# Two more items of a linear-attention and MLP kernel in float32 on unsplit weights, and six weight splits moved to later steps

## The chip, the cores and the metric

The kernel runs on one core of a Trainium2 chip. The metric is the device time of one execution in microseconds (us), lower is better. Five engines of the core are spoken of: PE (matrix products), DVE (elementwise and reductions), ACT (activation functions, copies), POOL and SP (here mostly issuing DMAs). Each works through its own list of instructions in order, and they wait for each other through semaphores.

## What is computed

The reference is a linear attention followed by a two-layer MLP without bias:

```python
q_s = softmax(q, over the head dimension)        # q, k, v: (8, 8, 576, 64)
k_s = softmax(k, over the sequence)
x   = q_s @ (k_s^T @ v)                          # per batch and head, then (4608, 512)
h   = x @ w_in                                   # w_in (512, 2048)
g   = h * erf(softplus(h))
out = g @ w_out                                  # w_out (2048, 512), out float32
```

The softmax subtracts the maximum and adds 1e-9 to the sum. The weights arrive as float64 and are decoded to float32 in the kernel.

## The kernel before

**Items.** The tokens are taken in four pairs of batches. Each pair has 1152 tokens, which are three blocks of 384, so there are twelve blocks. The hidden width of 2048 is taken in four groups of 512. One block with one group is an *item*: 48 items, numbered in the order of the list `seq` (line 893), block by block and, inside a block, group 0 to 3. So items 0 to 3 are block 0, items 4 to 7 are block 1, items 8 to 11 are block 2. An item consists of tokens that the author writes as letters: `m` the first product (x with w_in), which leaves H; `T` softplus, `G` erf and `U` the product of both with H, which leave g; `I` and `O` the split of g into two float16 parts; `M` the second product (g with w_out), which adds into three accumulator banks o0 to o2 per block. After a block's last item the banks are copied out (`ob`) and stored.

**Two ways of multiplying.** Items 0 to 3 (`n < NG`, NG is 4) use float32 matmuls on the decoded weights as they are: `mm1_32` (line 975) does sixteen of 384 columns into the PSUM banks pX, pY, pZ, pX, copied out by ACT (line 989), and `mm2` does twelve of 512 columns at line 1061. All later items use float16 parts: every operand is a high part and a low part, and a product is hi times hi, hi times lo and lo times hi. The first product of these items (`mm1`, line 922) is in addition a seven-product scheme for 2 by 2 blocks: seven products, `prod` (line 939), of twelve matmuls with 192 columns each at line 946, put together by four DVE operations (lines 958, 960, 968, 971) and three ACT copies (963, 965, 973). Its tokens are in four steps m*n*.0 to m*n*.3. The second product is 36 matmuls of 512 columns at line 1070.

**Splits.** For that the weights are split once. There are eight jobs (`JOBS`), numbered 0 to 7: w_in group 0, w_in 1, w_out 0, w_in 2, w_out 1, w_in 3, w_out 2, w_out 3. `D` decodes a job into a staging place; `Z` (`wscales`, line 251) computes the scales once all jobs are decoded; `S` (`wsplit`, line 300) and `R` (`wsplit_sums`, line 324) write the float16 parts. A part is made by `split2` (line 293): ACT writes the high part (line 294), then DVE the low part (line 295). For a w_in job S makes two such pairs and then four subtractions on DVE (line 320) in the staging place, and R two more pairs from the sums. A staging place of job j lies in the tile of job j+2, so job j+2 can be split only when job j is done; jobs 6 and 7 are staged in a spare x tile (`sg`) and in `rw`. The token block x of block 1 and later is split in the same way by `finish` (line 370, tokens `f`): an even f makes the parts of x itself, an odd f makes four subtractions (line 386) in place and then two pairs, into the tile `x7`.

**Order.** Up to item 3 and the first splits the order of the tokens is written out in `ORDER`; after it a loop over n from 4 emits `U` of item n-1, the four `m` of item n with `I`, `O` of item n-1 and `M` of item n-2 between them, the splits that the table `SPLITS` lists for n, and then `T` and `G` of item n. `A` and `pace` advance the attention of the coming batches by one step. The recording layer may place instructions of one engine in a somewhat different order than the tokens; each engine then works through its list strictly in that order. Items 0 to 3 are scaled by 1 in softplus (line 1014); later ones by `unit` (line 992), and `gmul` (line 1020) multiplies by GA, made in `wscales`.

## Time and profile before

| | us |
|---|---|
| three timed runs | 852.46, 854.15 (median), 856.45 |
| the profiled execution's own time | 854.95 |
| its span, first to last instruction | 852.8 |
| PE busy in the span | 812.2 |
| DVE busy | 640.0 |
| ACT busy | 506.1 |

The profile is one execution. A row of a timeline has the start in us from the span's start, the length in us, engine, line, operation, output and inputs with the buffer numbers left out, shape, type and count; neighbouring instructions of one kind stand in one row, and what ended an idle stretch just before the row stands in brackets. A float32 matmul leaves two records, so x8 in a row are four matmuls. The start of the next row, and not a row's own length, tells how fast an engine went on, since lengths overlap a little.

### The profile page before, as it was taken

What the parts mean: (1) busy time and instruction counts of PE and PEld (TensorE: products, weight loads), DVE (VectorE), ACT (ScalarE), POOL (GpSimd) and SP (SyncE); (2) the same over time, 40 slices, a digit from 0 to 9 for tenths busy, and PEclk for the clock granted to TensorE, in tenths of its full rate; (3) what the DMA queues carried; (4) which work ended last, traced back from release to release, by engine and by line L of the source; (5) the groups of instructions that cost most, each with busy time, mean ns of one, the idle gap of its engine ahead of it and who ended that gap; (6) DMA issues with size and microseconds to landing.
All of it is one profiled execution on the core that took longest, in us unless ns stands there. A gap on an engine that the chain in (4) does not pass through costs nothing.

```text
span 852.8 us, 15390 instructions
## 1 busy us (share of the span) xinstructions
PE 812.2 (95%) x6464; PEld 557.9 (65%) x6464; DVE 640.0 (75%) x913; ACT 506.1 (59%) x636; POOL 18.1 (2%) x37
## 2 busy tenths in 40 slices
PE   3999996799999999999999999999999999999996
PEld 2655546567766677676776677676776776777672
DVE  6999699998888778876886768876876557554543
ACT  2697677757585467556755467456665565543532
POOL 2101100000000000000000000000000000000000
PEclk9999998899999999999999999999999999999999
DMA  9975820031217212511062212511041000100100
GB/s 271 404 176 175 201 63 26 1 89 34 71 44 137 50 51 50 128 41 26 14 150 55 63 38 61 120 38 26 21 92 13 30 10 1 38 1 1 38 1 38
DMA packets 141348, 61.55 MB, mean 72 GB/s; under 512 B 130528, under 2 KB 132576, under 8 KB 141280
## 3 DMA queue, kind: packets, MB, share of 16 engines
q1 hardware_dynamic: 139104, 52.18, 24.9%
q0 software_dynamic: 2176, 8.39, 2.9%
q8 instruction: 51, 0.84, 0.4%
q14 instruction: 17, 0.14, 0.1%
HBM read 45.09 MB, written 9.44 MB: 64 GB/s over the span
## 4 chain that ended last, share of the span: by engine, by line
PE 64%; DVE 20%; ACT 6%; DMA 4%; issue 3%; SPq 2%; POOL 0%; ACTq 0%; DVEq 0%
PE o L1070 31%; PE pX L946 16%; PE pZ L946 8%; PE pY L946 3%; DVE G L1025 2%; ACT G L342 2%; ACT L342 2%; DVE wt L295 2%; SPq L407 2%; PE x L652 2%; PE kv L540 2%; DVE H L1042 1%; DMA vbuf<-in_v_dram 1%; DMA wt<-in_moe_w_out_dram 1%; DVE wt L214 1%
## 5 line engine op out<-in xcount | busy, mean ns | idle before, releaser
L1070 PE MATMUL o<-wt,H 128*128 128x512 f16 x1584 | 365.6, 379 | 1.9 <-DVE H L1038 1.3
L946 PEld LDWEIGHTS <-wt 128*128 128x128 f16 x3696 | 312.1, 99 | 44.1 <-issue 17.4
L1070 PEld LDWEIGHTS <-H 128*128 128x128 f16 x1584 | 152.5, 98 | 157.5 <-DVE H L1038 1.8
L946 PE MATMUL pX<-x,wt 128*128 128x192 f16 x2112 | 207.2, 249 | 11.9 <-DVE H L968 5.3
L342 ACT ACT_TABLE_LOAD x105 | 134.7, 1283 | 6.2 <-DVE U L996 2.4
L1025 DVE SCALAR_TENSOR_TENSOR G<-G,small,H 128x1536 f32<-128x1536 f32 x44 | 79.9, 1816 | 48.3 <-ACT G L342 48.0
L973 ACT COPY H<-pX 128x384 f32<-128x384 f32 x44 | 20.9, 476 | 147.6 <-PE pX L946 145.1
L946 PE MATMUL pZ<-x,wt 128*128 128x192 f16 x1056 | 104.6, 247 | 0.0
L342 ACT ACTIVATE G<-H,U 128x768 f32<-128x768 f32 (+1 forms) x60 | 72.8, 1231 | 22.1 <-DVE H L971 21.5
L1042 DVE TENSOR_TENSOR H<-G,H 128x1536 f16<-128x1536 f32 x44 | 77.2, 1754 | 1.0
L342 ACT ACTIVATE G<-G 128x1536 f32<-128x1536 f32 x48 | 71.2, 1484 | 0.5
L946 PE MATMUL pY<-x,wt 128*128 128x192 f16 x528 | 51.7, 246 | 1.4 <-DVE H L958 1.4
L441 ACT ACTIVATE x<-x 128x384 f32<-128x384 f32 (+1 forms) x52 | 17.7, 387 | 58.1 <-PE x L652 55.7
L971 DVE TENSOR_TENSOR H<-pZ,H 128x384 f32<-128x384 f32 x44 | 24.2, 549 | 31.4 <-PE pZ L946 31.4
L958 DVE COPY H<-pY 128x384 f32<-128x384 f32 x44 | 24.3, 552 | 25.7 <-PE pY L946 25.7
L294 ACT ACTIVATE x<-x 128x768 f16<-128x768 f32 (+1 forms) x44 | 33.0, 762 | 16.5 <-DVE x L386 15.8
L1038 DVE CAST H<-G 128x1536 f16<-128x1536 f32 x44 | 42.0, 955 | 0.9
L295 DVE SCALAR_TENSOR_TENSOR x<-x,x 128x768 f16<-128x768 f32 (+1 forms) x44 | 37.3, 849 | 3.6 <-ACT x L294 3.5
L1086 DVE TENSOR_SCALAR ob<-o,V 128x512 f32<-128x512 f32 x29 | 21.7, 747 | 21.6 <-PE o L1070 21.5
L960 DVE TENSOR_TENSOR H<-pX,H 128x384 f32<-128x384 f32 x44 | 24.3, 553 | 13.2 <-PE pX L946 12.7
L452 DVE TENSOR_REDUCE q_m<-q 128x16 f32<-128x1024 f32 x14 | 17.0, 1215 | 18.2 <-DMA q<-in_q_dram 18.1
L968 DVE TENSOR_TENSOR H<-pX,H 128x384 f32<-128x384 f32 x44 | 24.2, 550 | 6.0 <-PE pX L946 5.9
(180 smaller groups left out, 791.4 us busy)
## 6 DMA issues: line engine op xcount, KB each, us to landing
out_dram<-ob SPq DMA_DIRECT2D x32, 256.0 KB, 2.3
vbuf<-in_v_dram SPq DMA_DIRECT2D x60, 128.0 KB, 3.3
q<-in_q_dram SPq DMA_DIRECT2D x56, 128.0 KB, 3.2
k<-in_k_dram SPq DMA_DIRECT2D x56, 128.0 KB, 3.3
wt<-in_moe_w_out_dram POOLq DMA_DIRECT2D x5, 1024.0 KB, 8.7
wt<-in_moe_w_in_dram SPq DMA_DIRECT2D x4, 1024.0 KB, 10.7
wt<-in_moe_w_out_dram SPq DMA_DIRECT2D x2, 1024.0 KB, 15.5
H_raw<-in_k_dram SPq DMA_DIRECT2D x2, 512.0 KB, 4.7
```

Of the source, the lines that this page charges most:

```text
L294: nc.scalar.activation(hi, src, AF.Copy, scale=s)
L295: nc.vector.scalar_tensor_tensor(lo, src, s, hi, op0=ALU.mult, op1=ALU.subtract)
L342: i = nc.scalar.activation(out_, in_, func, **kw)
L946: nc.tensor.matmul(o, w[wl][:, c, a * P:(a + 1) * P], x[:, xl, xi, c, :], start=(new and a == 0 and c == 0 and i == 0), stop=(c == 1 and i ...
L958: nc.vector.tensor_copy(C[0, 0], bank2("Y"))
L960: add(C[0, 0], bank2("X"), C[0, 0], op=ALU.add)
L968: add(C[1, 1], bank2("X"), C[1, 1], op=ALU.add)
L971: add(C[0, 1], bank2("Z"), C[0, 1], op=ALU.add)
L1025: nc.vector.scalar_tensor_tensor(flat(s["G"]), flat(s["G"]), GA[:, g:g + 1], flat(s["H"]), op0=ALU.mult, op1=ALU.mult,)
L1038: nc.vector.tensor_copy(flat(s["gh"]), flat(s["G"]))
L1042: nc.vector.tensor_tensor(flat(s["gl"]), flat(s["G"]), flat(s["gh"]), op=ALU.subtract)
L1070: nc.tensor.matmul(o, s[gt][:, a, ts_], w[wl][:, a, :], start=(first_ and a == 0 and i == 0), stop=(last_ and a == FG - 1 and i == 2),)
```

## The change

Items 4 and 5, the first two of block 1, are now groups 2 and 3 instead of 0 and 1, and both of their products are done in float32 on the unsplit weights (`N32 = 6`); items 6 and 7 are groups 0 and 1 in float16 parts. Softplus of items 4 and 5 is scaled by the batch's `ux`, and their product with H by one new scalar GA32. Such items have no `I` and `O`. The first products of item 4 start before `Z`. Only splits S0, R0, S1, R1 are left in `ORDER`; S2 and S4 come in the loop at n = 6, S6, f2, f3, S3 and R3 at n = 7, S5 and R5 at n = 8, S7 at n = 9. The guard in `wsplit` now asks only that job j-2 is split.

```diff
--- before.py
+++ after.py
@@ -36,11 +36,14 @@
     m0.0 m0.1 D0.0.1 D0.1.1 D1.0 D1.1 m0.2 m0.3 T0 G0 Q0
     D2.0 A m1.0 D2.1 m1.1 U0 m1.2 m1.3 T1 G1 Q1 A A D3.0 M0.0 D3.1 M0.1 M0.2 Q2 U1 A A
     m2.0 D4.0 m2.1 D4.1 m2.2 m2.3 T2 G2 Q3 A A D5.0 M1.0 D5.1 M1.1 M1.2 U2 A A Q4 D6.0
-    m3.0 D6.1 m3.1 D7.0 m3.2 D7.1 m3.3 T3 G3 A A A A A A A A A A Q5 U3 Q6 Q7 Z S0 R0 f0 f1
-    M2.0 M2.1 M2.2 M3.0 M3.1 M3.2 S1 R1 S2
+    m3.0 D6.1 m3.1 D7.0 m3.2 D7.1 m3.3 T3 G3 A A A A A A A A A A Q5 U3 Q6 Q7
+    M2.0 M2.1 M2.2 m4.0 m4.1 Z m4.2 m4.3 T4 G4 M3.0 f0 M3.1 M3.2 S0 R0 m5.0 m5.1 U4 m5.2 m5.3
+    T5 G5 f1 S1 R1
 """
 
-SPLITS = {4: "S3 R3 S4", 5: "S5 R5 S6", 6: "S7"}
+
+N32 = 6
+SPLITS = {6: "S2 S4", 7: "S6 f2 f3 S3 R3", 8: "S5 R5", 9: "S7"}
 
 SHARES = [2.51, 0, 0.16, 0.09, 1.58, 2.43, 1.12, 0.26, 0.29, 0.04, 0.78, 1.12, 0.16]
 LEAD = 2.0
@@ -92,6 +95,7 @@
     make_identity(nc, ident)
     small = cp.tile([P, 48], F32, name="small")
     VW = small[:, 3:4]
+    GA32 = small[:, 32:33]
 
     vbuf = cp.tile([P, 4, TM, D + 1], F32, name="vbuf")
     nc.gpsimd.memset(vbuf[:, :, :, D:], 1.0)
@@ -289,20 +293,24 @@
         nc.vector.tensor_scalar(
             VW, m[:, 2:3], m[:, 3:4], 2.0**20, op0=ALU.mult, op1=ALU.mult
         )
+        nc.vector.tensor_scalar(
+            GA32, m[:, 0:1], m[:, 1:2], 2.0**-20, op0=ALU.mult, op1=ALU.mult
+        )
 
     def split2(src, hi, lo, s):
         nc.scalar.activation(hi, src, AF.Copy, scale=s)
         nc.vector.scalar_tensor_tensor(lo, src, s, hi, op0=ALU.mult, op1=ALU.subtract)
 
-    nsplit = [0]
+
+    split = set()
 
     def wsplit(jn):
 
 
         which, g = wjobs[jn]
         s = w_s[which][:, g:g + 1]
-        assert "all" in wready and not raws and jn == nsplit[0]
-        nsplit[0] += 1
+        assert "all" in wready and not raws and (jn < 2 or jn - 2 in split)
+        split.add(jn)
         if which == "out":
             split2(stg.pop(jn), whalf(jn, 0), whalf(jn, 1), s)
             wdone(jn)
@@ -890,7 +898,10 @@
         )]
 
 
-    seq = [(p, bk, g) for p in range(NP) for bk in range(NBK) for g in range(NG)]
+    seq = [
+        (p, bk, (g + 2 * (p == 0 and bk == 1)) % NG)
+        for p in range(NP) for bk in range(NBK) for g in range(NG)
+    ]
     N = len(seq)
     blk_items = {}
     for n, it in enumerate(seq):
@@ -975,8 +986,8 @@
     def mm1_32(n, a):
 
         s = st[n]
-        jn = wjobs.index(("in", n))
-        w, x = stg[jn].rearrange("p (c f) -> p c f", c=4), xbl[0]
+        jn = wjobs.index(("in", seq[n][2]))
+        w, x = stg[jn].rearrange("p (c f) -> p c f", c=4), xbl[n // NG]
         if a == 0:
             s["H"] = ch.tile([P, FG, T], F32, tag="H", bufs=3, name=f"H_{n}")
         b = "XYZX"[a]
@@ -1010,7 +1021,7 @@
         for o, w, b in spans(n):
             h, sp = s["H"], s["G"]
             h, sp = (flat(t) if w == T else t[:, :, o:o + w] for t in (h, sp))
-            u = 1.0 if n < NG else unit(b, g)
+            u = 1.0 if n < NG else bat[b]["ux"] if n < N32 else unit(b, g)
             act(sp, h, AF.Softplus, chain=in_chain(n), scale=u)
 
     def erf(n):
@@ -1022,11 +1033,13 @@
         if n < NG:
             nc.vector.tensor_tensor(flat(s["G"]), flat(s["G"]), flat(s["H"]), op=ALU.mult)
             return
+        assert "all" in wready
         nc.vector.scalar_tensor_tensor(
-            flat(s["G"]), flat(s["G"]), GA[:, g:g + 1], flat(s["H"]),
+            flat(s["G"]), flat(s["G"]), GA32 if n < N32 else GA[:, g:g + 1], flat(s["H"]),
             op0=ALU.mult, op1=ALU.mult,
         )
-        assert "all" in wready
+        if n < N32:
+            return
 
         hl = flat(s["H"]).bitcast(F16)
         s["gh"], s["gl"] = (
@@ -1055,7 +1068,7 @@
         o = acc[tt]
         jn = wjobs.index(("out", g))
         ts_ = slice(tt * P, (tt + 1) * P)
-        if n < NG:
+        if n < N32:
             w = stg[jn].rearrange("p (a e) -> p a e", a=FG)
             for a in range(FG):
                 nc.tensor.matmul(
@@ -1130,7 +1143,7 @@
         elif c == "Z":
             wscales()
         elif c == "m":
-            (mm1_32 if x[0] < NG else mm1)(*x)
+            (mm1_32 if x[0] < N32 else mm1)(*x)
             emitted.add(("m", *x))
         elif c == "M":
             mm2(*x)
@@ -1148,7 +1161,7 @@
     w_even = sum(SHARES[:9]) + NC4 * sum(SHARES[11:])
     w_odd = w_even + sum(SHARES[9:11])
     per_pair = w_even + w_odd
-    n1 = NG + 3
+    n1 = NG + 4
 
     def pace(at_n):
 
@@ -1165,18 +1178,18 @@
 
     for o in ORDER.split():
         tok(o)
-    fi = [2]
+    fi = [4]
     FIN = 2
-    for n in range(4, N + 2):
+    for n in range(N32, N + 2):
         m0, m1, m2 = n < N, n - 1 < N, n - 2 < N
         if m1:
             tok(f"U{n - 1}")
         for i in range(4):
             if m0:
                 tok(f"m{n}.{i}")
-            if 4 < n <= N and i < 2:
+            if N32 < n <= N and i < 2:
                 tok(f"{'IO'[i]}{n - 1}")
-            if m0 and n % NG == FIN and i < 2 and x_next[0] < NP * NBK:
+            if m0 and n % NG == FIN and n > N32 and i < 2 and x_next[0] < NP * NBK:
                 tok(f"f{fi[0]}")
                 fi[0] += 1
             if m2 and i < 3:
```

On PE, from the second product of item 3 on, the list before is this. Names carry the item or batch in their first number: pY_4 is a bank of item 4, o_0_2 the third accumulator of block 0; x7_1 is the split x of block 1, wt0 holds the split of job 0; each matmul of line 946 has its own LDWEIGHTS.

```order
L1061 MATMUL o_0_2_462<-rw_86,G_3_693 128x512 x4
L946 LDWEIGHTS wt0_91
L946 MATMUL pY_4_886<-x7_1_825,wt0_91 128x192
...
L946 MATMUL pX_4_900<-x7_1_825,wt0_91 128x192
...
L946 MATMUL pZ_4_914<-x7_1_825,wt0_91 128x192
...
L946 MATMUL pY_5_1002<-x7_1_825,wt1_92 128x192
```

And with the change, where x_1 is the unsplit x of block 1, wt5 and wt7 hold the staged w_in groups 2 and 3, and sg_6 the staged w_out group 2:

```order
L996 MATMUL pZ_4_2_839<-x_1_139,wt5_96 128x384 x4
L1074 MATMUL o_0_0_449<-rw_86,G_3_693 128x512 x4
L1074 MATMUL o_0_1_457<-rw_86,G_3_693 128x512 x4
L1074 MATMUL o_0_2_462<-rw_86,G_3_693 128x512 x4
L996 MATMUL pX_5_0_894<-x_1_139,wt7_98 128x384 x4
L996 MATMUL pY_5_1_900<-x_1_139,wt7_98 128x384 x4
L996 MATMUL pZ_5_2_907<-x_1_139,wt7_98 128x384 x4
L996 MATMUL pX_5_3_913<-x_1_139,wt7_98 128x384 x4
L957 MATMUL pY_6_945<-x7_1_862,wt0_91 128x192
...
L957 MATMUL pX_6_959<-x7_1_862,wt0_91 128x192
...
L1074 MATMUL o_4_0_973<-sg_6_653,G_4_851 128x512 x4
```

The float16 products of block 1 that stood right behind item 3 now stand behind the float32 first products of items 4 and 5, and between the second and the third of item 6's seven products (the next row is pX_6 once more, with the last part of x7_1) stands a third of item 4's second product.

On ACT, the two high parts of x7_1 that an odd f makes stood before, among the first splits:

```order
L294 ACTIVATE wt1_92<-wt3_94,small_81 128x512
L1080 COPY ob_3_0_854<-o_0_0_449 128x512
L294 ACTIVATE x7_1_825<-x_1_139 128x768
L294 ACTIVATE wt0_91<-wt2_93,small_81 128x1024
...
L1080 COPY ob_3_1_861<-o_0_1_457 128x512
```

The second of them is in the place of the three dots' end, ahead of every softplus of block 1. With the change they stand around item 5's softplus and erf; the dots leave out a table load and the second high part:

```order
L1000 COPY H_5_893<-pX_5_3_913 128x384
L350 ACT_TABLE_LOAD
L350 ACTIVATE G_5_919<-H_5_893,x0_u_311 128x4x192
L350 ACTIVATE G_5_919<-H_5_893,x1_u_634 128x4x192
L301 ACTIVATE x7_1_862<-x_1_139 128x768
...
L350 ACTIVATE G_5_919<-G_5_919 128x1536
...
L976 COPY H_6_944<-pX_6_959 128x2x192
L301 ACTIVATE wt6_97<-sg_6_653,small_81 128x2048
```

So both stand behind the copy of the last first product of item 5, and the second also behind its erf.

On DVE, the last low part of x7_1 stood before ahead of the split of job 1 and of the first evacuation of item 4:

```order
L295 SCALAR_TENSOR_TENSOR x7_1_825<-x_1_139,x7_1_825 128x768
L295 SCALAR_TENSOR_TENSOR wt1_92<-wt3_94,small_81,wt1_92 128x1024
L295 SCALAR_TENSOR_TENSOR wt1_92<-wt3_94,small_81,wt1_92 128x512
L958 COPY H_4_885<-pY_4_886 128x2x192
L320 TENSOR_TENSOR wt3_94<-wt3_94 128x2x256
L295 SCALAR_TENSOR_TENSOR wt2_93<-wt4_95,small_81,wt2_93 128x2048
```

With the change it stands behind G_5, which is `gmul` of item 5; the dots leave out the rest of f1's subtractions, its first low part and four subtractions of job 3:

```order
L302 SCALAR_TENSOR_TENSOR wt4_95<-wt6_97,small_81,wt4_95 128x2048
L969 COPY H_6_944<-pY_6_945 128x2x192
L394 TENSOR_TENSOR x_1_139<-x_1_139 128x2x192
L971 TENSOR_TENSOR H_6_944<-pX_6_959,H_6_944 128x2x192
...
L1037 SCALAR_TENSOR_TENSOR G_5_919<-G_5_919,small_81,H_5_893 128x1536
L302 SCALAR_TENSOR_TENSOR x7_1_862<-x_1_139,x7_1_862 128x768
L302 SCALAR_TENSOR_TENSOR wt6_97<-sg_6_653,small_81,wt6_97 128x2048
```

The last low part of x7_1 has moved from before block 1's products to behind item 5's whole chain of softplus, erf and gmul.

## The prediction

> **What bounds the kernel now.** I read the page first. PE is busy nearly throughout, and the slices show where it isn't.
>
> ```profile
> PE 812.2 (95%) x6464; PEld 557.9 (65%) x6464; DVE 640.0 (75%) x913; ACT 506.1 (59%) x636; POOL 18.1 (2%) x37
> PE   3999996799999999999999999999999999999996
> DVE  6999699998888778876886768876876557554543
> PEclk9999998899999999999999999999999999999999
> ```
>
> After the start, PE falls below nine tenths only in the seventh and eighth of 40 slices (21.3 us each, so about 128 to 171 us), there its granted clock falls too, and DVE is full. Everywhere else the time is PE's own work. So the change is worth what it recovers in that stage, less the PE work that it adds. The busy times by stretch say more:
>
> ```profile
> core 0: us, PE busy (x) PEld busy (x) DVE busy (x) ACT busy (x) POOL busy (x), PEclk, DMA share, GB/s
> 112.03:128.29 16.26, 15.27 (x46) 7.29 (x45) 16.06 (x41) 11.19 (x18) 0.96 (x1) 1.00 0.24 64
> 128.29:200.55 72.26, 58.48 (x540) 46.10 (x539) 69.49 (x101) 50.40 (x55) 0.63 (x2) 0.91 0.16 38
> 140.12:147.30 7.18, 5.66 (x37) 5.05 (x37) 7.17 (x10) 5.44 (x5) 0.00 (x0) 0.52 0.01 3
> 158.80:164.30 5.50, 5.48 (x32) 4.55 (x32) 5.50 (x9) 1.01 (x2) 0.00 (x0) 0.50 0.00 0
> ```
>
> From 128.29, where block 1's first float16 matmul starts, to 200.55, DVE is busy 69.49 of 72.26 us and PE idles 13.8; in two pieces the clock is half. The PE timeline has the waits in brackets, and DVE ends nearly all of them:
>
> ```profile
> 113.19 0.65 PE L261 MATMUL ws_in<-ident,small 128*128 128x128 f32 x4 [0.99 <-DVE small L255]
> 117.99 10.46 PE L1061 MATMUL o<-rw,G 128*128 128x512 f32 x24
> 128.29 1.15 PE L946 MATMUL pY<-x,wt 128*128 128x192 f16 x12
> 136.71 1.15 PE L946 MATMUL pX<-x,wt 128*128 128x192 f16 x12 [1.79 <-DVE H L960]
> 158.82 2.08 PE L946 MATMUL pX<-x,wt 128*128 128x192 f16 x12 [2.84 <-DVE H L968]
> ```
>
> The evacuations that PE waits for stand in DVE's list behind the splits.
>
> How much of the 72.26 us is work? The counts of the three kinds of matmul in that stretch, and the speed of each in a dense stretch later:
>
> ```profile
> 128.29:200.55 72.26, 38.34 (x374) 34.99 (x374) 0.91 0.16 38
> 128.29:200.55 72.26, 17.68 (x72) 6.80 (x72) 0.91 0.16 38
> 128.29:200.55 72.26, 3.93 (x80) 3.13 (x80) 0.91 0.16 38
> 260.02 0.69 PE L540 MATMUL kv<-vbuf,k 128*64 128x65 f32 x16
> 261.34 1.17 PE L946 MATMUL pX<-x,wt 128*128 128x192 f16 x12
> 268.51 1.15 PE L946 MATMUL pX<-x,wt 128*128 128x192 f16 x12
> 269.50 2.75 PE L1070 MATMUL o<-wt,H 128*128 128x512 f16 x12
> 272.09 1.15 PE L946 MATMUL pZ<-x,wt 128*128 128x192 f16 x12
> 241.34 0.60 PE L519 MATMUL kB<-ident,km 128*128 128x128 f32 x4
> 241.77 1.15 PE L946 MATMUL pX<-x,wt 128*128 128x192 f16 x12
> ```
>
> The first three rows are lines 946, 1070 and 540. Twelve of line 946 go on in 0.99 us (268.51 to 269.50), twelve of line 1070 in 2.59, forty kv records in 1.32, four transposes in 0.43. So the work is 374 x 0.99/12 = 30.9, 72 x 2.59/12 = 15.5, 2 x 1.32 = 2.6, and about 1.4 for thirteen transposes: 50.4 us. The stage loses 72.3 - 50.4 = 21.8 us with unrounded terms, and 0.99 more before it, at ws_in.
>
> **What the change adds on PE.** One float32 first product, and float16 ones beside it:
>
> ```profile
> 90.26 2.75 PE L985 MATMUL pY<-x,wt 128*128 128x384 f32 x8
> 92.84 2.74 PE L985 MATMUL pZ<-x,wt 128*128 128x384 f32 x8
> 95.42 2.74 PE L985 MATMUL pX<-x,wt 128*128 128x384 f32 x8
> ```
>
> A quarter of an item takes 2.58 us, so an item 10.32; in float16 it is seven times 0.99, 6.93. A second product is the x24 row at 117.99, 10.30 us to the next row; in float16 three times 2.59, 7.77. So each of the two items costs 20.62 where it cost 14.70, and both together 11.8 us more. All of it is on PE, and nothing hides it.
>
> **What it takes from DVE.** Two items lose four evacuations, a cast and a subtraction each:
>
> ```profile
> 158.22 0.54 DVE L968 TENSOR_TENSOR H<-pX,H 128x384 f32<-128x384 f32 x1
> 158.69 0.94 DVE L1038 CAST H<-G 128x1536 f16<-128x1536 f32 x1
> 160.03 1.74 DVE L1042 TENSOR_TENSOR H<-G,H 128x1536 f16<-128x1536 f32 x1
> ```
>
> That is 2 x (4 x 0.54 + 0.94 + 1.74) = 9.7 us of DVE. It has a price only through PE's waits, and so isn't a term of its own. ACT's evacuations go from three to four per item, next to nothing. The splits stay eight; their cover is now the 30.9 us of PE work that need no split: the first products of 4 and 5 (20.6) and item 3's second (10.3). The wait of 0.99 at ws_in goes, since item 4's first product stands there and needs only x; its third bank waits for the DVE reduction of ws_out, which I place just in time (a queries' load ahead of it in DVE's list could cost 0 to 1.7).
>
> **What is late next.** Here a new wait is added, and the order shows it. The odd f works in place on block 1's x, so it must wait for item 5's last first-product matmul. Its second high part stands on ACT behind item 5's softplus and erf, and its second low part on DVE behind item 5's gmul. Item 6's third product needs it, and everything on PE is queued behind that product. The chain's pieces:
>
> ```profile
> 183.22 1.58 ACT L294 ACTIVATE x<-x 128x768 f16<-128x768 f32 x2 [1.92 <-DVE x L386]
> 193.03 1.76 ACT L342 ACTIVATE G<-H,U 128x768 f32<-128x768 f32 x2
> 195.11 0.48 ACT L965 COPY H<-pX 128x384 f32<-128x384 f32 x1 [0.32 <-PE pX L946]
> 195.61 1.28 ACT L342 ACT_TABLE_LOAD   x1
> 196.90 1.48 ACT L342 ACTIVATE G<-G 128x1536 f32<-128x1536 f32 x1
> 198.42 1.82 DVE L1025 SCALAR_TENSOR_TENSOR G<-G,small,H 128x1536 f32<-128x1536 f32 x1 [0.17 <-ACT G L342]
> 128.25 0.95 DVE L295 SCALAR_TENSOR_TENSOR x<-x,x 128x768 f16<-128x768 f32 x1
> 133.24 2.35 DVE L295 SCALAR_TENSOR_TENSOR wt<-wt,small,wt 128x2048 f16<-128x2048 f32 x1
> ```
>
> From the end of item 5's first product: copy 0.48, table 1.28, softplus 1.76, first high part 0.79, table to the start of gmul 2.81 (195.61 to 198.42), gmul 1.82, low part 0.95: 9.9 us. Meanwhile PE has two float16 products (1.98) and a third of item 4's second product (3.43), 5.4 us. So PE waits 4.5. DVE could make it longer: behind the first of f1's four subtractions stand the low part of S4 (2.35) and two evacuations before the last subtraction, which ends about 0.5 us after the softplus. I take 4.8 us of idle (bounds 4.4 and 6).
>
> Such a gap costs more than itself. After the 2.84 us at 158.82 the clock was 0.50 for 5.5 us: 2.7 us of work lost. I take the same 2.7 (0 if the clock holds, 3.4 as at 140.12, 7.18 x 0.48). [...]
>
> Behind that wait I followed the three lists on, each operation at its row's length. DVE and ACT stay ahead of PE through the late splits, by a few us mostly; two small waits come up near the first products of block 2, 0.4 at a bank and 0.4 at the attention's queries. I take 0.8 for them, with 0 and 4 as bounds. Block 2's products find their split x ready some 8 us early by that reckoning.
>
> **Sum.** Recovered 21.8 + 1.0; paid 11.8 + 4.8 + 2.7 + 0.8 = 20.1. Gain 2.7 us. The profiled execution took 854.95 (span 852.8 and 2.15 around it), so it would take 852.25; it lies 0.8 above the median of 854.15, and on the median the forecast is 851.45, I say 851.4. With the terms' likely errors (each about 1 to 2 us, not all one way) its own range is 848.6 to 854.2.
>
> **Rivals.** *The clock holds or the chain is covered.* If PE's idle falls so across the clock's decision that it isn't halved, or waits and work overlap better, the gain is 5.4: 848.7. For it: a wait of 0.99 at 113.19 left the clock at 1.00. Against it: two of two stretches with long waits were halved. I give it 0.17.
>
> *A second wait of the same kind, slower than before.* With the change S6, R3, part of S5 and f2 stand in DVE's list ahead of the subtraction of the keys' maximum of batch 2, and the kv products on PE, and all behind them, wait for the exp of these keys. Ahead of it in DVE's list since S6's low part are about 14 us: S6 2.35, low parts from R3, S5 and f2 some 5, evacuations, subtractions and a reduction 7. By my reckoning there are 16.4 us for them, and the keys' chain has about 1 us of slack, so it decides from about 3.4 us of delay on: 8 us late is 4.6 idle and again 2.7 at the halved clock. The gain of 2.7 turns into a loss of 1.9 without the clock and 4.6 with it: 856.0 to 858.8. For it: DVE was busy 69.49 of 72.26 us in this stage before, and the change puts six splits there later. Against it: 9.7 us of DVE work are gone. I give it 0.19, two thirds of that at the upper end.
>
> *The table load brings a drain.* If each switch of tables also waited for ACT to run empty, about as long as the load itself takes (1.28), the two in the chain above would lengthen the wait by 2.6 and leave almost no gain, 854.0. Against it: copy, load and erf stand at 195.11, 195.61 and 196.90, back to back. [...] I give it 0.02.
>
> *The loss only moves.* The order changes, but DVE, which by my reckoning ends item 7 about 8 us later against PE's place than before, hands the rest of the gain back in waits of block 2: about 854.1, chance 0.07. The forecast's own case has 0.55.
>
> **Numbers.** About 0.5% (4.3 us) is what a measurement of this kernel can tell from no change: faster is below 849.9, slower above 858.4. Faster: the first rival, 0.17, and a fifth of the forecast's case, 0.12, together 0.29. Slower: the upper two thirds of the second rival, 0.13. Within: 0.58. The range 847.0 to 857.5 leaves out that upper part and a few hundredths at the low end.
>
> **What would show it.** Right: 128 f32 records at the line of `mm1_32` and 96 at that of `mm2` become 192 and 144; the PE timeline has no wait from 112 to the end of item 5's first products near 148; then one wait of 4 to 6 us, ended by the low part of x7_1 on DVE, and a clock of 0.50 for some 5 us behind it; after it nothing above 1 us to block 2. Wrong: that wait missing or under 3 us with the clock at 1.00 (first rival), a wait at the kv products of batch 2 ended by the exp of k (second), a gap ahead of the table loads (third), or new waits between 200 and 260 us (fourth).

## The result: 846.8 us, below the range

| | median, us (lowest to highest, runs) | ratio to before, 95% interval |
|---|---|---|
| before, beside it | 854.02 (852.46 to 856.45, 4) | |
| changed | 846.8 (846.17 to 847.5, 4) | 0.9913 [0.9887, 0.9939] |
| changed, a second time (e8) | 845.6 (844.91 to 846.46, 4) | 0.9909 [0.9895, 0.9922] |
| changed, a third time (e16) | 845.85 (845.2 to 847.16, 5) | 0.9911 [0.9898, 0.9924] |

Each ratio is to runs of the kernel before on the same chip, beside the runs of its row. The change gains 7.2 us where 2.7 was forecast, and the time lies just outside the range, 0.2 us under its low end. The profiled execution took 847.39 with a span of 845.4, 7.4 us shorter than before's. The page of the changed kernel:

```profile
PE 817.5 (97%) x6336; PEld 554.3 (66%) x6336; DVE 631.9 (75%) x900; ACT 506.6 (60%) x638; POOL 18.1 (2%) x37
PE   3999999999999999999999999999999999999996
DVE  6899689998998869867877769867876657553543
PEclk9999999999999999999999999999999999999999
```

The two low slices of PE are gone, and with them the low clock. PE now has more to do (817.5 against 812.2 us) and still ends earlier. The busy times of the two stretches that answer to 112.03:128.29 and 128.29:200.55, split where the float16 products of block 1 begin:

```profile
112.46:149.21 36.75, 35.91 (x109) 19.21 (x108) 33.62 (x66) 26.40 (x35) 0.96 (x1) 1.00 0.14 40
149.21:190.88 41.67, 41.26 (x330) 27.98 (x329) 40.22 (x58) 32.42 (x36) 0.63 (x2) 1.00 0.15 33
149.21:190.88 41.67, 17.16 (x192) 1.00 0.15 33
```

The third row is line 957 alone, the float16 first products. PE is idle 0.84 us in the first stretch and 0.41 in the second, where it idled 13.8 us before. DVE is still busy nearly all the time (33.62 + 40.22 of 78.42 us), but PE hardly waits for it. How much of this is gained at equal work? At 190.88 the changed kernel has 192 records of line 957 behind it, which with the two items that no longer use that line (168) is 14 short of the 374 that before had at 200.55; that is 14 x 0.99/12 = 1.2 us, and with about 0.5 of transposes it owes 1.7. So before needed 88.5 us for what now takes 78.4 + 1.7 = 80.1: a gain of 8.4 us there. The span is 7.4 shorter: 0.4 had been lost ahead of this stretch, which starts at 112.46 instead of 112.03, and 0.6 is given back behind it.

The PE timeline where the prediction placed its new wait; o<-rw is item 3's second product and o<-sg item 4's, both in float32, and line 957 is item 6's first product:

```profile
125.94 2.82 PE L996 MATMUL pZ<-x,wt 128*128 128x384 f32 x8 [0.84 <-DVE wse_in L272]
128.59 10.46 PE L1074 MATMUL o<-rw,G 128*128 128x512 f32 x24
138.89 2.74 PE L996 MATMUL pX<-x,wt 128*128 128x384 f32 x8
...
149.21 1.15 PE L957 MATMUL pY<-x,wt 128*128 128x192 f16 x12
150.20 1.15 PE L957 MATMUL pX<-x,wt 128*128 128x192 f16 x12
151.19 3.62 PE L1074 MATMUL o<-sg,G 128*128 128x512 f32 x8
...
155.31 1.07 PE L957 MATMUL pX<-x,wt 128*128 128x192 f16 x11 [0.41 <-DVE x L302]
156.21 1.91 PE L1074 MATMUL o<-sg,G 128*128 128x512 f32 x4
157.96 0.25 PE L957 MATMUL pZ<-x,wt 128*128 128x192 f16 x1
158.04 1.91 PE L1074 MATMUL o<-sg,G 128*128 128x512 f32 x4
159.79 1.07 PE L957 MATMUL pZ<-x,wt 128*128 128x192 f16 x11
...
205.15 0.59 PE L660 MATMUL x<-asc,kvbd 128*128 128x512 f16 x2 [1.62 <-DVE asc L639]
```

And what DVE and ACT did there, from the copy of item 5's last first product to the two low parts of x7_1 (line 302):

```profile
149.41 0.48 ACT L1000 COPY H<-pX 128x384 f32<-128x384 f32 x1 [0.94 <-PE pX L996]
149.91 1.28 ACT L350 ACT_TABLE_LOAD   x1
151.21 1.76 ACT L350 ACTIVATE G<-H,x_u 128x768 f32<-128x768 f32 x2
152.88 0.84 ACT L301 ACTIVATE x<-x 128x768 f16<-128x768 f32 x1
...
156.43 0.83 ACT L301 ACTIVATE x<-x 128x768 f16<-128x768 f32 x1
...
152.30 0.55 DVE L394 TENSOR_TENSOR x<-x 128x384 f32<-128x384 f32 x1
...
154.30 0.96 DVE L302 SCALAR_TENSOR_TENSOR x<-x,x 128x768 f16<-128x768 f32 x1
...
156.56 1.82 DVE L1037 SCALAR_TENSOR_TENSOR G<-G,small,H 128x1536 f32<-128x1536 f32 x1
158.29 0.95 DVE L302 SCALAR_TENSOR_TENSOR x<-x,x 128x768 f16<-128x768 f32 x1
```

The chain has the length that was forecast: from the end of item 5's first products at 149.21 to the end of the second low part at 159.24 it takes 10.0 us, where 9.9 was reckoned. But item 6's third product (the row at 155.31) starts 0.05 us behind the *first* low part, which ends at 155.26, 4 us before the second. The half that it needs (j = 1 in the code of `finish`) is the one that is made early: its two subtractions are the second and third of the four, the third is the row at 152.30, and at 152.88, ahead of item 5's erf, ACT begins its high part. What needs the late half is the product after it (pZ), and ahead of its bulk at 159.79 stand two pieces of item 4's second product, 1.8 us each. So the late half is hidden as well.

The waits of PE in the changed kernel from 110 to 260 us (us in total, times, longest):

```profile
PE x L660 <- DVE asc L639: 1.6, 1, 1.6
PE kB L527 <- DVE km L518: 1.2, 1, 1.2
PE pZ L996 <- DVE wse_in L272: 0.8, 1, 0.8
PE pX L957 <- DVE x L302: 0.4, 1, 0.4
```

The evacuations of the float16 first products (H), which held PE up most in before's timeline, are gone from the list. Four short waits are left, 4.0 us together; the first two lie behind 190.88.

### The profile page after: what moved, and what is told of

It is laid out like the page before. It is cut to its first block, busy times and chain, and to the rows that moved or that the text cites. A ratio compares the mean times of both kernels' runs of the same rounds, so it can differ in the third digit from the quotient of the medians.

```text
span 845.4 us, 15123 instructions
## 1 busy us (share of the span) xinstructions
PE 817.5 (97%) x6336; PEld 554.3 (66%) x6336; DVE 631.9 (75%) x900; ACT 506.6 (60%) x638; POOL 18.1 (2%) x37
## 4 chain that ended last, share of the span: by engine, by line
PE 66%; DVE 16%; ACT 10%; DMA 3%; issue 3%; SPq 1%; POOL 0%; ACTq 0%; DVEq 0%; POOLq 0%
PE o L1083 28%; PE pX L957 15%; PE pZ L957 8%; PE o L1074 4%; ACT G L350 3%; PE pY L957 3%; ACT L350 3%; DVE G L1037 2%; PE kv L548 2%; DVE H L1055 2%; DMA q<-in_q_dram 1%; PE x L660 1%; SPq L415 1%; ACT wt L301 1%; DVE wt L302 1%
## 5 line engine op out<-in xcount | busy, mean ns | idle before, releaser
L1083 PE MATMUL o<-wt,H 128*128 128x512 f16 x1512 | 347.4, 379 | 1.8 <-DVE H L1051 1.3
L957 PEld LDWEIGHTS <-wt 128*128 128x128 f16 x3528 | 294.0, 98 | 29.3 <-issue 5.6
L1083 PEld LDWEIGHTS <-H 128*128 128x128 f16 x1512 | 145.9, 98 | 150.8 <-DVE H L1051 1.8
L957 PE MATMUL pX<-x,wt 128*128 128x192 f16 x2016 | 193.9, 246 | 1.8 <-ACT H L976 0.7
L957 PE MATMUL pZ<-x,wt 128*128 128x192 f16 x1008 | 98.2, 246 | 0.0
L350 ACT ACTIVATE G<-H,U 128x768 f32<-128x768 f32 (+1 forms) x56 | 69.3, 1255 | 22.1 <-DVE H L982 21.5
L1055 DVE TENSOR_TENSOR H<-G,H 128x1536 f16<-128x1536 f32 x42 | 73.8, 1756 | 1.0
L957 PE MATMUL pY<-x,wt 128*128 128x192 f16 x504 | 48.4, 246 | 0.0
L1099 DVE TENSOR_SCALAR ob<-o,V 128x512 f32<-128x512 f32 x29 | 21.7, 749 | 21.9 <-PE o L1083 21.8
L996 PE MATMUL pX<-x,wt 128*128 128x384 f32 x96 | 33.9, 488 | 0.0
L971 DVE TENSOR_TENSOR H<-pX,H 128x384 f32<-128x384 f32 x42 | 23.3, 555 | 13.3 <-PE pX L957 12.5
```

The costliest lines, as they stand in the source:

```text
L350: i = nc.scalar.activation(out_, in_, func, **kw)
L957: nc.tensor.matmul(o, w[wl][:, c, a * P:(a + 1) * P], x[:, xl, xi, c, :], start=(new and a == 0 and c == 0 and i == 0), stop=(c == 1 and i ...
L971: add(C[0, 0], bank2("X"), C[0, 0], op=ALU.add)
L996: nc.tensor.matmul(ph[:, :T], w[:, c, a * P:(a + 1) * P], x[:, c, :], start=(c == 0), stop=(c == NC4 - 1),)
L1055: nc.vector.tensor_tensor(flat(s["gl"]), flat(s["G"]), flat(s["gh"]), op=ALU.subtract)
L1083: nc.tensor.matmul(o, s[gt][:, a, ts_], w[wl][:, a, :], start=(first_ and a == 0 and i == 0), stop=(last_ and a == FG - 1 and i == 2),)
```

## The experiments

The theory after this result: the float32 items are cover. They give PE work that needs no split while DVE works off the splits, so the loss of the stage goes; they cost 5.9 us each; and the new wait on the late half didn't come because item 4's second product lies over it and the third product needs the early half. The rivals: the gain comes from putting six splits later; it comes from the DVE work that the two items no longer have; or the new wait was never as dear as reckoned.

**e1, the cover held back.** Item 4's second product (x[0] == 4 is its item) is made to stand behind the last matmuls of both products of item 6 that need the parts of an odd f (`held4`, X and Z for pX and pZ), and item 7's first product behind the last of item 6's pX. The step m6.1 is moved up to stand right behind m6.0. The main part of the edit:

```diff
-            mm2(*x)
+            with ExitStack() as es:
+                if x[0] == 4:
+                    es.enter_context(tc.issue_after(held4["X"].ins))
+                    es.enter_context(tc.issue_after(held4["Z"].ins))
+                mm2(*x)
```

> The changed kernel, with the second product of item 4 held behind the third and fourth of item 6's seven first products, so that PE has nothing to lay over the splits of x. Theory (the forecast wait did not come because item 4's second product and the order of the two halves of f1 cover it): PE now waits 4 to 7 us between its second and fifth product of item 6, ended by the low parts of x7_1, the granted clock falls to about 0.5 for some us behind it, and the time is 6 to 10 us above the changed kernel, 853 to 857. Rival (the clock holds at this place whatever the wait, since float32 work goes ahead of it): the waits alone, 4 to 6 us, clock 1.00, 851 to 853. Rival (PE has slack there): under 849.

Measured: 848.74 us, ratio 0.9939 [0.9924, 0.9954]: some 2 us over the changed kernel, not 6 to 10. That is the number of the last rival (under 849), but not its reason, since PE does wait and its clock does fall, only less than was meant. PE's rows there, and its granted clock (us, busy, PEclk):

```profile
152.36 0.24 PE L957 MATMUL pX<-x,wt 128*128 128x192 f16 x1 [1.97 <-DVE x L394]
153.02 0.65 PE L527 MATMUL kB<-ident,km 128*128 128x128 f32 x4 [0.42 <-DVE km L518]
153.88 1.60 PE L957 MATMUL pX<-x,wt 128*128 128x192 f16 x11 [0.21 <-DVE x L302]
155.89 0.32 PE L957 MATMUL pZ<-x,wt 128*128 128x192 f16 x1 [0.40 <-ACT x L301]
```

```profile
154.00:155.00 1.00, 1.00 (x10) 0.63 0.06 16
...
157.00:158.00 1.00, 1.00 (x11) 0.67 0.00 0
```

The waits are 3.0 us together, and the clock was halved for 3.4 us: means of 0.63 and 0.67 are 0.74 and 0.66 us at 0.50, and the two us between, left out here, are at 0.50 throughout. That cost about 1.5 us of work. Of the 4.5, some 2 show in the end; the 1.6 at the attention's queries isn't in this run's list of waits. The recording layer had laid transposes (kB) ahead and had put the second low part ahead of item 5's gmul on DVE (156.00 and 156.87 there), so that the wait was shorter than the edit was meant to make it. This run doesn't price the predicted situation; e15 below does.

**e2 and e3, how many items.** e2 does all four items of block 1 in float32, e3 one. The tables change with it; the eight weight splits stay, and e2 needs no split x for block 1. The main lines of both edits:

```diff
-N32 = 6
-SPLITS = {6: "S2 S4", 7: "S6 f2 f3 S3 R3", 8: "S5 R5", 9: "S7"}
+N32 = 8
+SPLITS = {6: "S2", 7: "f2 f3 S3 R3", 8: "S4 S5 R5", 9: "S6", 10: "S7"}
...
+N32 = 5
+SPLITS = {5: "S1 R1 S2", 6: "S3 R3 S4", 7: "S6 f2 f3", 8: "S5 R5", 9: "S7"}
```

> The changed kernel with all four items of block 1 in float32, in the groups' first order, no split x for block 1, and every split later still. Theory (PE bounds, and a float32 item costs 5.9 us more than a float16 one): 11.8 us more PE work, of which at most the 2 to 3 us of small waits left in the changed kernel come back, so 9 to 12 us above it, 856 to 859. Rival (DVE is still the bound in this stage, so taking 10 us of evacuations, casts, subtractions and the split of x from it pays again): at or below the changed kernel, 843 to 848.

> The changed kernel with only item 4 in float32 (group 3 first, then groups 0, 1, 2 in float16), the splits spread over n = 5 to 9 as the groups need them. Theory (float32 items are cover for the splits): 5.9 us less PE work, but only half the cover: DVE has jobs 0, 1, 2 and the split of x to do before items 5 and 6, PE waits come back, 5 to 12 us with part of the clock, so 846 to 853. Rival (the late placing alone brings the gain and the float32 work is only a cost): about 5.9 us below the changed kernel, 840 to 842.

Measured: e2 857.82, ratio 1.0051 [1.0034, 1.0068]; e3 847.54, ratio 0.9931 [0.9914, 0.9948]. e3's kernel ran once more under the label e7, a single run of 846.92.

> The kernel with one float32 item once more, for one look: the same time as its first run, 847 to 849, and waits spread over the same places.

What is left of the stage in e3, by the same window in before, in e3, in the changed kernel and in e2 (us, PE busy, PEld, DVE, ACT, POOL, PEclk):

```profile
110.00:260.00 150.00, 133.26 (x1058) 93.37 (x1056) 140.65 (x219) 104.55 (x128) 1.59 (x3) 0.95 0.20 49
```

```profile
110.00:260.00 150.00, 141.91 (x1081) 94.18 (x1080) 139.54 (x218) 105.72 (x132) 2.22 (x5) 1.00 0.20 48
```

```profile
110.00:260.00 150.00, 145.92 (x1031) 95.58 (x1030) 138.48 (x215) 106.55 (x134) 2.22 (x5) 1.00 0.21 50
```

```profile
110.00:260.00 150.00, 146.54 (x792) 87.94 (x791) 114.25 (x175) 98.76 (x121) 1.59 (x3) 1.00 0.17 43
```

PE's idle time goes from 16.7 us without such an item to 8.1 with one and 4.1 with two, and with one the clock already holds (1.00). The four items of e2 leave 3.5 us, about as much as two, so two more items bring nothing more and cost their price: e2 is 1.0051 - 0.9913 = 1.38% of 854, 11.8 us, slower than the changed kernel. That is the 2 x 5.9 us that the prediction worked out from the row lengths. With that price the gains give what was recovered: 0.69% or 5.9 + 5.9 = 11.8 us with one item, 7.4 + 11.8 = 19.2 with two. One item and two end about 1.5 us apart, since the second item recovers only 7.4 for its price of 5.9; that is within the two intervals, so these runs don't tell one item from two for certain. Three items were not run.

**e4 and e12, the splits early.** e4 is the changed kernel with S2 to S5, R3 and R5 in the order list, ahead of item 6, and S6 and S7 earlier in the loop; e12 puts the splits of e3 one step earlier. The edit of e4:

```diff
-    T5 G5 f1 S1 R1
+    T5 G5 f1 S1 R1 S2 S3 R3 S4 S5 R5
...
-SPLITS = {6: "S2 S4", 7: "S6 f2 f3 S3 R3", 8: "S5 R5", 9: "S7"}
+SPLITS = {6: "S6 f2 f3", 7: "S7"}
```

> The changed kernel with both float32 items kept but S2, S3, R3, S4, S5, R5 moved back ahead of item 6, S6 and the split of block 2's x to n = 6, S7 to n = 7. Theory (where the splits stand decides, because evacuations queue behind them on DVE): PE waits ended by DVE come up between item 5's first products and item 7, 2 to 6 us, so 849 to 853. Rival (only the DVE work that float32 items save counts, and the place of the splits does not): within 1 us of the changed kernel, 846 to 848.

> One float32 item with its splits earlier: S1, R1, S2 before the loop, then S3 R3 S4, S6 f2 f3, S5 R5 and S7 at n = 5 to 8. Theory (the place of the splits hardly matters, since early splits changed the two-item kernel by 1 us at most): within 2 us of the other kernel with one item, 845 to 849. Rival (with less cover, early splits delay the evacuations): 850 to 853.

Measured: e4 845.72, ratio 0.9906 [0.9889, 0.9922], against 0.9909 to 0.9913 for the changed kernel; e12 848.27, 0.9936 [0.9917, 0.9955], against 0.9931 of e3. The place of the splits in the program makes no difference that these runs can show. The first rival falls, and with it what e4's text puts on record as its theory (849 to 853).

**e5, DVE relieved in the kernel before.** No float32 item is added. Instead the low parts of the four w_out jobs are not computed but set to zero on POOL, which leaves out part of the computation (the terms of the second product with the low part of w_out) and takes 4 x 2.35 = 9.4 us off DVE:

```diff
-            split2(stg.pop(jn), whalf(jn, 0), whalf(jn, 1), s)
+            nc.scalar.activation(whalf(jn, 0), stg.pop(jn), AF.Copy, scale=s)
+            nc.gpsimd.memset(whalf(jn, 1), 0.0)
```

> The kernel before, with the low parts of the four w_out jobs not computed but set to zero by POOL, so that DVE has four operations of 2.3 us less (9.4 us) in the stage of the splits; nothing else changes, and no float32 item is added. Theory (PE's waits in block 1 are DVE's backlog, so they shrink by what is taken from it): 8 to 12 us below the kernel before with the clock's share, 841 to 846. Rival (only PE work that needs no split covers the waits, DVE's load as such does not matter, since each evacuation waits behind some other split or behind ACT's high parts): within 3 us of the kernel before, 850 to 853.

Measured: 846.6, ratio 0.9913 [0.9898, 0.9927], as much as the change brings, though a little less than the 8 to 12 us expected. So it is DVE's backlog in this stage that PE pays for in the kernel before: 9.4 us less of it are worth 7.3 us. PE's two longest waits in that run:

```profile
PE o L1071 <- DVE H L1039: 4.3, 2, 3.7
PE pX L947 <- ACT H L966: 1.9, 2, 1.6
```

It still waits for evacuations (line 966) and for the split of g (line 1039): by other means the same time is won, with less recovered and nothing paid on PE.

**e6, DVE work put back.** The changed kernel, with the casts and subtractions of items 4 and 5 done on DVE though nothing uses them:

```diff
-    T5 G5 f1 S1 R1
+    I4 O4 T5 G5 f1 S1 R1
...
-        if n < N32:
-            return
...
-            if N32 < n <= N and i < 2:
+            if N32 <= n <= N and i < 2:
```

> The changed kernel with the cast and the subtraction of items 4 and 5 done on DVE again though nothing reads them (5.4 us more DVE work between the splits). Theory (with 31 us of PE work that needs no split, DVE has room): PE waits grow by 0 to 3 us, so 0 to 3 above the changed kernel, 846 to 849. Rival (the DVE work that the change saves is where its gain comes from): 5 us above it, 851 to 853.

> The changed kernel again beside the others on the same chip: 0.989 to 0.994 of the kernel before.

Measured: e6 846.43, ratio 0.9918 [0.9905, 0.9932]; beside it e8, the changed kernel again, 845.6, 0.9909 [0.9895, 0.9922]. Reckoned at 5.4 us, the extra work costs 0.8, within the intervals. So the change doesn't live on the DVE work that the items drop: with two items of cover DVE has the slack to do it. In the kernel before the same DVE has none (e5). The second rival falls for the 5.4 us that were put back; the 4.3 us of evacuations that the two items also lose (2 x 4 x 0.54) were not.

**e9, e10, e11, the low parts on POOL.** If DVE's backlog is the loss, an idle engine could take some of it. The low parts of the w_out jobs are made on POOL, in the kernel before (e9), in e3 (e10) and in the changed kernel (e11):

```diff
-            split2(stg.pop(jn), whalf(jn, 0), whalf(jn, 1), s)
+            src = stg.pop(jn)
+            nc.scalar.activation(whalf(jn, 0), src, AF.Copy, scale=s)
+            nc.gpsimd.tensor_scalar_mul(src, src, s)
+            nc.gpsimd.tensor_tensor(whalf(jn, 1), src, whalf(jn, 0), op=ALU.subtract)
```

> The kernel before, with the low parts of the four w_out jobs made by POOL (scale in place, then subtract) instead of DVE; the output is the reference's, and no float32 item is added. Theory (DVE's backlog in the stage of the splits is what PE waits for): as when these low parts are left out, 6 to 8 us below the kernel before, 845 to 848, if POOL's pair takes under 10 us and nobody waits for it. Rival (POOL is late, or slows DVE while both work): 850 or more, with PE waits ended by POOL.

> One float32 item and the low parts of the w_out jobs on POOL. Theory (cover and relief of DVE add up until the 21.8 us of loss are used up): 5.9 us of gain from one item as measured, and the waits left in it shrink, 841 to 845. Rival (the relief is worth nothing once a float32 item covers the splits): 846 to 848.

> The changed kernel with the low parts of the w_out jobs on POOL. Theory (two float32 items already cover the splits; 5.4 us more on DVE cost it only 0.8): at most 1.5 us below the changed kernel, 844 to 846. Rival (relief of DVE is worth as much here as in the kernel before): 838 to 840.

Measured: 871.58 (1.0207 [1.018, 1.0233]), 866.02 (1.0137 [1.0112, 1.0161]) and 867.13 (1.0157 [1.0136, 1.0177]): 17 to 22 us worse than the same kernels without it, where all three theories had 841 to 848 us; only e9's rival allowed for it. POOL and DVE in e11:

```profile
159.86 4.06 POOL L318 TENSOR_TENSOR wt<-wt,wt 128x2048 f16<-128x2048 f32 x1
...
159.92 5.09 DVE L302 SCALAR_TENSOR_TENSOR wt<-wt,small,wt 128x1024 f16<-128x1024 f32 x1
...
165.40 1.27 DVE L302 SCALAR_TENSOR_TENSOR wt<-wt,small,wt 128x1024 f16<-128x1024 f32 x1
```

The same DVE operation took 1.27 us with POOL at rest (165.40) and 5.09 when it started 0.06 us behind a POOL operation; it ended 1.09 us after that one. From 120 to 200 us of e11 the twelve low parts of 128x1024 took 2054 ns on average and the sixteen subtractions of 128x512 1314, in the changed kernel 1280 and 690 in the same window. That is some 19 us more for DVE (an estimate from these means and counts), against 9.4 us of low parts that it no longer makes. So the relief turned into a load. More is said of it in the last section.

**e13 and e14, the halves swapped.** To make the third product of item 6 wait for a late half, the two pairs that an odd f writes for block 1 are put in the other order; e14 also holds the second third of item 4's second product behind the first four of item 6's products. The part that both share:

```diff
+                if i == 1 and j == 1:
+                    for p in prev:
+                        es.enter_context(tc.issue_after(p))
-                split2(x[:, :, Th * j:Th * j + Th], hi, lo, 1.0)
+                prev = split2(x[:, :, Th * j:Th * j + Th], hi, lo, 1.0)
```

> The changed kernel with the two halves of block 1's odd f forced into the order that the forecast assumed: the half that item 6's third product does not need comes first, the needed one second. The recording layer then puts both behind item 5's erf and lays more of item 4's second product ahead of the products that need them. Theory (the forecast failed because the needed half comes first; cover takes up what is left): PE waits 1 to 3 us in one place near 158 us, the clock may fall, 0 to 4 us above the changed kernel, 846 to 850. Rival (the forecast's wait is real once the halves are in this order, cover or not): 4.5 us of idle and the clock at half, 7 us above, 853 to 855.

> The same, with the second third of item 4's second product held behind item 6's first four products, so that less cover is left. Theory: a wait of 2 to 5 us between 155 and 162 us ended by a low part of x7_1, then a granted clock of 0.5 for 3 to 6 us: 3 to 7 us above the changed kernel, 849 to 853. Rival (other work fills it): within 2 us of the run with the swapped halves alone.

Measured: e13 845.31, ratio 0.991 [0.9897, 0.9923]; e14 845.61, 0.9916 [0.9902, 0.9931]. Both equal the changed kernel, and e14's theory (849 to 853) falls. PE in e14:

```profile
150.31 7.06 PE L1079 MATMUL o<-sg,G 128*128 128x512 f32 x16
157.56 0.24 PE L962 MATMUL pZ<-x,wt 128*128 128x192 f16 x1 [0.19 <-ACT x L301]
```

The swap does a little more than it says. Both halves now stand behind item 5's erf and gmul (their high parts from 156.68 on, their low parts from 158.84 on in e14), and the product laid third is pZ, which reads the half that is now made first. So both halves are late. But the recording layer laid eight float32 matmuls ahead of the third product instead of four, 6.9 us of cover (e13's list has the same eight), and the wait is 0.19; in e14 item 7's first product and a piece of item 5's second then fill the place behind it. So late halves alone cost nothing as long as there is cover to be moved.

**e15, both taken away.** The halves swapped as in e13, and all of item 4's second product held back as in e1. Beside it e16, the changed kernel.

> The changed kernel with the half of block 1's split x that needs no subtraction of the other half made first, so that the half of item 6's third product is the one behind item 5's softplus, erf and product with H, and with all of item 4's second product laid behind item 6's first three products that need it. Theory (cover, not the order of the halves, spared the wait): with no float32 work left between the second product of item 6 and the late half, PE idles 6 to 9 us there (the chain of 9.9 us from the end of item 5's first product, less two float16 products of 0.99 and two short transposes), the clock falls to 0.50 behind it for 3 to 6 us, and the time is 7 to 11 us above the changed kernel, 852 to 857. Rival (the wait would have been small in any case, the chain being shorter than reckoned, or later work makes it good): wait under 3 us, within 3 us of the changed kernel.

> The changed kernel again, for a comparison on the same chip: 845 to 848, ratio to the kernel before 0.990 to 0.992 by either theory.

Measured: e15 854.65, ratio 1.0009 [0.9999, 1.0019]; e16 845.85, 0.9911 [0.9898, 0.9924]. The difference is 0.98% of 854, 8.4 us, inside the expected 7 to 11. PE in e15, and its clock:

```profile
148.53 0.60 PE L519 MATMUL kT<-ident,asc 128*128 128x128 f32 x4
151.82 0.65 PE L532 MATMUL kB<-ident,km 128*128 128x128 f32 x4 [2.69 <-DVE km L523]
155.77 0.32 PE L962 MATMUL pZ<-x,wt 128*128 128x192 f16 x1 [3.29 <-ACT x L301]
156.50 0.32 PE L962 MATMUL pX<-x,wt 128*128 128x192 f16 x1 [0.41 <-ACT x L301]
158.11 1.92 PE L962 MATMUL pZ<-x,wt 128*128 128x192 f16 x11 [1.28 <-DVE x L302]
159.82 1.96 PE L962 MATMUL pX<-x,wt 128*128 128x192 f16 x11
```

```profile
152.00:153.00 1.00, 0.48 (x4) 0.67 0.00 0
153.00:154.00 1.00, 0.00 (x0) 0.50 0.00 0
...
162.00:163.00 1.00, 1.00 (x3) 0.71 0.00 0
```

Here is the situation that was predicted, except that the prediction left a third of item 4's second product as cover and e15 leaves none. It costs what such a wait was said to cost: 2.69 + 3.29 + 0.41 + 1.28 = 7.7 us of idle, and eleven matmuls in 1.71 us (158.11 to 159.82) where the changed kernel needs 0.90 (159.79 to 160.69), because the clock is at half from about 152.3 to 162.6; from 158.11 on that is 4.5 us at half speed, 2.2 us of work. Together 9.9; less the waits of 0.4 and, at the queries, 1.6 that the changed kernel has and e15 hasn't, and with 0.6 at the kv products that only e15 has, 8.5 are left for the 8.4 that were measured. The whole gain of the change is gone. So the price was right, and the cover and the early half are what spared it.

## Why the prediction was wrong

The sum was 22.8 recovered, 20.1 paid. Term by term:

- **The float32 work, 11.8 us: right.** 192 records stand at line 996 and 144 at line 1074, as named; item 3's second product takes 10.30 us (128.59 to 138.89) and item 5's first 10.32 (138.89 to 149.21). e2 measured 11.8 for two more items.
- **The loss of the stage, 21.8, and the wait at ws_in, 1.0: right in kind, 1.4 us too large.** Hardly any idle time is left up to 190.88 (0.84 + 0.41) and the clock is 1.00, so all that could be recovered was. At equal work 8.4 were gained, while 22.8 - 11.8 - 1.25 would be 9.75; the difference means that the stage's work was set 1.4 us too low. That the cover recovers it is shown by e3 and the change, which take the idle time away in two steps, and e5 shows that it is DVE's backlog; e4 shows that the later place of the splits isn't what recovers it. One reading was too strong: of the waits from 128.29 to 200.55 in the kernel before, 14.0 us, DVE ended 9.0, which isn't nearly all; copies of ACT ended 3.3 and a DMA 1.7.
- **The new idle wait, 4.8: the step that failed.** The prediction said of the second low part of x7_1: "Item 6's third product needs it, and everything on PE is queued behind that product." It doesn't need it. The code writes the two halves in the order j = 0, j = 1, and I took the late one for the one that the third product reads. But the recording layer makes the half j = 1 first, since its subtractions are done first, and that is the half that the third product reads. The wait is 0.41. The next product, which does need the late half, found two more pieces of item 4's second product ahead of it, where the prediction counted on a third of that product as the only cover. e14 shows the cover alone to be enough; e1 shows that the early half without it leaves some 2 us. The chain itself was timed rightly (10.0 against 9.9), and e15 shows that the wait comes, and is dear, when both are taken away.
- **The half clock, 2.7: not paid,** since the wait before it didn't come. Its size was fair: e1 lost about 1.5 us to it and e15 about 2.2.
- **Small waits, 0.8: too low.** 0.84 came at the third bank of item 4 (for wse_in), inside the 0 to 1.7 given for it; 1.62 at the attention's queries near block 2, where 0.4 was said, and 1.2 at kB. Part of these stood in before too (kB 1.4, kv 1.0). Of the 8.4 - 7.4 = 1.0 us that the span lacks, 0.4 was lost ahead of 112.46, and what comes after 190.88 gives back 0.6.

With the failed step and its clock taken out, 22.8 - 11.8 - 0.8 would have been a gain of 10.2; the overrated loss and the small waits bring it to 7.4. The range failed in the same place: the first rival took away either the clock's part or some of the wait and stopped at 848.7. Both gone at once, 4.8 + 2.7 less to pay, was never priced, though the covered chain that the rival names would take both.

Of the rivals, the covered chain is what happened, with 0.17. A second wait at the keys of batch 2 didn't come: the kv rows have no wait. The drain at table loads didn't show: in the rows above the load ends at 151.19 and the softplus starts at 151.21. That the loss only moves is refuted up to 0.6 us.

One thing stays open. e3's window from 110 to 260 shows 8.6 us less idle and the full clock, which less its price of 5.9 would be worth more than the 5.9 us that it gains; part of what is missing lies in its start (14.73 us of PE work in the first 30 us, 15.39 in before). The single run of the same kernel under e7 has a span of 845.0, 7.8 us shorter than before's, and 6.9 us of idle time in that window; so e3's profiled execution (848.89, its median is 847.54) is one of the longer ones, but the rest of the difference was not traced.

## What to carry to other kernels

Work that needs none of what a backlogged engine prepares is worth its own price and more if it is laid over that backlog: here 11.8 us of extra matrix work hid some 19 us of waiting and halved clock, and more of it doesn't pay once the idle time is used up: two items end some 1.5 us ahead of one, within the intervals, and four are 11.8 us behind two. Before a new wait is priced, find out from the order, buffer by buffer, which half of a tile is made first and which consumer reads it, and what else the layer that orders the instructions could still move ahead; the rows of before give the length of the chain well, but not whether anybody stands behind it. And when a term is doubtful as a whole, the range has to reach to the sum without it.

## What the runs showed of the hardware

**DVE beside POOL.** In e9 and e11 POOL's scaling of 128x2048 float32 took 5.4 to 6.0 us and its subtraction 4.1 to 4.9. In e11 the low part of 128x1024 that started 0.06 us behind such a subtraction took 5.09 us instead of 1.27, as above. A DVE subtraction of 128x512 that took 0.68 us at 153.40 took 4.12 from 154.47 on, 0.6 us behind the start of a scaling, and ended 1.2 us before that scaling did (153.87 to 159.78). Across 120 to 200 us of e9 the sixteen subtractions of 128x512 took 1477 ns on average, in the kernel before 679. e5 has memsets on POOL in the place of both operations (1.80 to 2.56 us, with no input in their rows); it took 846.6 us, e9 871.58. One of the memsets, and the group of the subtractions in e9:

```profile
132.30 1.80 POOL L308 MEMSET wt<- 128x2048 f16 x1 [0.23 <-ACT wt L307]
```

```profile
L323 DVE TENSOR_TENSOR wt<-wt 128x512 f32<-128x512 f32 x16 | 23.6, 1477 | 0.0
```

**The clock fell after broken gaps too.** In e15 it fell at about 152.3 us, while the transposes ran that broke the idle time after 2.69 us; and in e1 at about 154.3, when the last gap of note, 1.97 us, was 1.9 us past. It came back after 3.4 us in e1, and in e15 4.5 us after steady work had begun. The lengths differ: it is at half from 140.38 to 147.20 and from 157.44 to 164.26 in the kernel before, from 154.26 to 157.66 in e1 and from 152.34 to 162.58 in e15 (the last two by the means of the rows above). These are 6.82, 6.82, 3.40 and 10.24 us, about two, two, one and three times the shortest, and the two stretches of the kernel before begin 17.06 us apart, about five times it. In the 3.41 us (half of 6.82) before each of these four falls PE was busy for 1.15, 1.15, 1.27 and 0.71 us. What decides where a stretch begins and ends was not shown.
